# Second-layer output products with the activations as stationary operand and the weights streamed

## The chip, the cores and the metric

The kernel runs on one core of one Trainium2 chip. The metric is the device time of one execution in microseconds, from its first to its last work on the core; the median of three runs is quoted. A program on one core has nothing to exchange with others, so the time is that of the five engines (TensorE, VectorE, ScalarE, GpSimd, SyncE) and their DMA transfers.

## What is computed

A windowed weighted sum over 7 tokens (the "attention"), then two dense layers over 8192 tokens of width 192, each with a hidden width of 2048.

```python
def _moe_ref(x, w_in, w_out):      # first layer
    h = x @ w_in                   # 8192 x 192 @ 192 x 2048
    g = h * np.cos(h)
    return g @ w_out               # 8192 x 2048 @ 2048 x 192

def _moe2_ref(x, w_in, w_out):     # second layer
    h = x @ w_in
    g = np.maximum(0.01 * h, h)
    return g @ w_out

x = attn_out.reshape(8192, 192)
x = _moe_ref(x, w_in1, w_out1)
return _moe2_ref(x, w_in2, w_out2)
```

The weights arrive as 64-bit floats, the activations as 32-bit floats. On the chip every operand of a product is split into a rounded high part and a low remainder ("hi", "lo"), and three products hi x hi, hi x lo, lo x hi are added, so that the sum keeps more bits than one product.

## The kernel before, in words

**Tiling.** The tokens stand in 16 blocks of 512 (four groups of 128, `Q = 4`). The hidden width stands in 16 chunks of 128 (`f`). In both layers activations lie transposed: features on partitions, 512 tokens along the free axis. TensorE is used as two halves of 64 rows (`SIDES`), called side 0 and side 1, each with its own products and weight loads.

**A chunk** (`chunk`, line 819) has 9 *hidden* products (`hidden`, L832: weights loaded, 512 tokens streamed, into one PSUM bank `h`) on the side given by the parity of `f`, then the activation (`acts`), which gives `hi` and `lo` of 128 x 512. In layer 2 that is Prelu in place in the bank (ScalarE, L898), a copy to `hi` (L293, or VectorE) and the difference to `lo` (VectorE, L311); after it the hidden bank is free. In layer 1 the steps are L867, L874, L879, L884 and a difference, most of them on GpSimd.

**Output products** (`project`, L842). A chunk's 128 hidden rows are the contraction; each side takes its 64. Per chunk and side there are five products of 512 columns: the weights `ohi`, `olo` (128 output features) and `or` (the remaining 64, high and low part side by side) are loaded and `hi` or `lo` of 512 tokens streamed. The sums over all 16 chunks stand in two banks per block, `m` and `r`. The result lies transposed, so in layer 2 `take` (line 922) copies the main sum to `om`, adds the halves of the rest to `s` through `sw`, and `back` issues 12 transposes on TensorE (`turn64`, L308) into two banks `po`, which four copies take to `osb`; one store writes the block.

**Order.** `seq` lists all chunks of both layers in pairs; two `streams` alternate at the start. Each side has its list of steps (`lists`): side 0 does the hidden products of pair p and then the output products of pair p - 2, side 1 the output products of pair p - 3 and then the hidden products of pair p. The loop at line 358 puts both lists into one program order, step by step. The two sides must not write one bank at the same time, so where a side turns to a bank that the other side wrote last, at least `APART` steps lie between and a wait (a nop on TensorE, in `piece`) on the end of a product `APART` steps back is put ahead. `Plan` then emits everything engine by engine by due times and costs; the pieces of TensorE's list stay in their order, and every other step goes where its engine is free.

**PSUM.** Eight banks of 128 x 512 float32: hidden banks (`hq`, up to `HELD = 6`), sums (two a block, of two blocks for a while at a change of block) and transposes (`tq`, two). A bank is handed on when its last reader is done.

**Weights** (`weights`, line 689). Four groups of four chunks per layer; each is loaded, taken apart from float64 by ScalarE, VectorE and GpSimd, and split (`ihi`, `ilo`, `ohi`, `olo`, `or`), in the order in which `seq` first needs them.

## Time and profile before

| | |
|---|---|
| median of three runs | 1197.27 us (1196.46 to 1198.04) |
| the profiled execution | 1196.44 us |
| its span, first to last instruction | 1194.6 us |
| TensorE products, busy | 1161.4 us, 97% |
| TensorE weight loads, busy | 1049.5 us, 88% |
| VectorE, ScalarE, GpSimd busy | 75%, 71%, 37% |
| mean granted TensorE clock | 0.988 of full speed |

All numbers but the first row come from one execution under the profiler. Product starts and load times are recorded; a product's end is modelled, and products overlap, so a busy TensorE is judged by the spacing of starts. `PE` is a product, `PEld` a weight load. "x8" behind a row of the timeline means that eight equal instructions were merged into it.

### The profile page before, as it was taken

To read this page: it belongs to the slowest core of one execution; us is meant where nothing else is said; L and a number is where in the kernel's file an instruction comes from. 1 tells how busy PE (TensorE), PEld (TensorE's weight loads), DVE (VectorE), ACT (ScalarE), POOL (GpSimd) and SP (SyncE) were. 2 spreads that over 40 slices of the span, in tenths; PEclk is the share of its full clock that TensorE was granted. 3 is DMA by queue.
4 is the path that set the end of the run, shared out by engine and by line. 5 is a ranking of instruction groups with operands and counts; after the bars stand their busy time and mean duration, and the time that the engine had idled before them with its cause. 6 is when DMAs were issued, how large, how long until landed. Compare 5 with 4: busy or idle time off the path is not lost.

```text
span 1194.6 us, 25907 instructions
## 1 busy us (share of the span) xinstructions
PE 1161.4 (97%) x10364; PEld 1049.5 (88%) x10364; DVE 892.5 (75%) x1356; ACT 852.4 (71%) x1554; POOL 440.3 (37%) x330
## 2 busy tenths in 40 slices
PE   6899799999999999999999999999999999999998
PEld 5677678888888899889998899989999899999997
DVE  7899797888868688786867778787787868746532
ACT  5798657886776767777676766867677676767653
POOL 4685732571432406143250613415052341504200
PEclk8899899999999999999999999999999999999999
DMA  6533420122020121202112120211212012020100
GB/s 180 157 97 89 131 76 15 41 61 54 27 57 18 47 54 63 54 11 62 29 47 55 47 54 2 75 42 48 54 47 54 1 47 54 15 54 15 28 1 27
DMA packets 31334, 62.46 MB, mean 52 GB/s; under 512 B 4276, under 2 KB 22194, under 8 KB 31216
## 3 DMA queue, kind: packets, MB, share of 16 engines
q1 hardware_dynamic: 31216, 60.82, 18.3%
q8 instruction: 82, 1.34, 0.5%
q14 instruction: 36, 0.29, 0.1%
HBM read 30.13 MB, written 6.29 MB: 30 GB/s over the span
## 4 chain that ended last, share of the span: by engine, by line
PE 90%; DVE 3%; DMA 2%; POOL 1%; ACT 1%; issue 1%; SPq 0%; ACTq 0%; DVEq 0%; POOLq 0%
PE ps L842 47%; PE ps L832 41%; PE ps L308 1%; DMA w00out<-in_moe_w_out 1%; DMA w00in<-in_moe_w_in 0%; DVE lo L311 0%; DMA w03in<-in_moe_w_in 0%; POOL ilo L311 0%; DMA x1r<-x1r 0%; ACT hi L293 0%; DVE g L874 0%; ACT g L879 0%; SPq L699 0%; DVE wt00out L754 0%; DVE wt10out L754 0%
## 5 line engine op out<-in xcount | busy, mean ns | idle before, releaser
L311 POOL TENSOR_TENSOR lo<-g,hi 128x512 fp32r<-128x512 f32 x240 | 335.0, 1399 | 517.4 <-ACT hi L293 461.4
L842 PE MATMUL ps<-hi,ohi 64*128 64x512 f32 x1024 | 402.6, 393 | 0.2 <-ACT hi L293 0.2
L842 PE MATMUL ps<-hi,olo 64*128 64x512 f32 x1024 | 398.7, 389 | 3.1 <-POOL olo L311 3.1
L842 PE MATMUL ps<-lo,ohi 64*128 64x512 f32 x1024 | 399.5, 390 | 1.2 <-DVE lo L311 0.6
L842 PE MATMUL ps<-lo,or 64*128 64x512 f32 x1024 | 398.5, 389 | 0.0
L842 PE MATMUL ps<-hi,or 64*128 64x512 f32 x1024 | 397.9, 389 | 0.0
L311 DVE TENSOR_TENSOR lo<-ps,hi 128x512 fp32r<-128x512 f32 x272 | 186.7, 689 | 150.6 <-ACT hi L293 146.1
L898 ACT ACTIVATE ps<-ps 128x512 f32<-128x512 f32 x256 | 148.9, 582 | 143.1 <-PE ps L832 103.0
L884 DVE TENSOR_TENSOR g<-ps,g 128x512 f32<-128x512 f32 x240 | 164.9, 688 | 73.1 <-ACT g L879 68.9
L832 PE MATMUL ps<-x1n,ihi 64*128 64x512 f32 x512 | 199.8, 390 | 2.4 <-DVE x0r L311 2.4
L842 PEld LDWEIGHTS ps<-hi,olo 64*128 64x128 f32 x1024 | 189.3, 185 | 13.8 <-POOL olo L311 3.5
L842 PEld LDWEIGHTS ps<-lo,ohi 64*128 64x128 f32 x1024 | 189.0, 185 | 13.4 <-POOL lo L311 1.7
L832 PE MATMUL ps<-x0n,ihi 64*128 64x512 f32 x512 | 198.9, 394 | 1.3 <-DVE lo L311 1.2
L832 PE MATMUL ps<-x1r,ihi 64*128 64x512 f32 x512 | 199.8, 390 | 0.0
L832 PE MATMUL ps<-x1s,ihi 64*128 64x512 f32 x512 | 198.9, 388 | 0.5 <-DMA x1s<-x1n 0.5
L842 PEld LDWEIGHTS ps<-hi,ohi 64*128 64x128 f32 x1024 | 189.4, 185 | 11.1 <-ACT hi L293 0.5
L832 PE MATMUL ps<-x0r,ihi 64*128 64x512 f32 x512 | 197.3, 389 | 1.8 <-DMA x0r<-x0r 1.8
L842 PEld LDWEIGHTS ps<-hi,or 64*128 64x128 f32 x1024 | 189.4, 185 | 10.8 <-POOL or L311 0.4
L842 PEld LDWEIGHTS ps<-lo,or 64*128 64x128 f32 x1024 | 189.2, 185 | 9.8
L832 PE MATMUL ps<-x0s,ihi 64*128 64x512 f32 x512 | 196.3, 387 | 0.4 <-DMA x0s<-x0n 0.4
L874 DVE SCALAR_TENSOR_TENSOR g<-g,ps 128x512 f32<-128x512 int32 x256 | 174.3, 682 | 26.0 <-ACT g L867 21.3
L879 ACT ACTIVATE g<-g 128x512 f32<-128x512 f32 x256 | 161.4, 632 | 42.8 <-DVE g L874 40.6
(228 smaller groups left out, 2634.9 us busy)
## 6 DMA issues: line engine op xcount, KB each, us to landing
xt<-in_x SPq DMA_DIRECT2D x12, 960.0 KB, 5.1
x1s<-x1n SPq DMA_DIRECT2D x32, 256.0 KB, 3.1
x0s<-x0n SPq DMA_DIRECT2D x30, 256.0 KB, 3.8
out<-osb SPq DMA_DIRECT2D x16, 384.0 KB, 2.7
x0r<-x0r SPq DMA_DIRECT2D x56, 64.0 KB, 3.0
x1r<-x1r SPq DMA_DIRECT2D x56, 64.0 KB, 2.6
smw<-in_weight_gen SPq DMA_DIRECT2D x3, 448.0 KB, 4.1
xt<-in_x SPq DMA_DIRECT2D x3, 384.0 KB, 4.2
```

Of the source, the lines that this page charges most:

```text
L308: nc.tensor.matmul(out, v, ident[r, r.start : r.stop], is_transpose=True, **{"start": True, "stop": True, **flags})
L311: eng[e].tensor_tensor(out=out, in0=a, in1=b.bitcast(F32), op=ALU.subtract)
L832: return nc.tensor.matmul(h(), w[rows, j, d], x()[rows, v], start=i == 0, stop=i == 8)
L842: return nc.tensor.matmul(to(), w[r, f % GF, :], v()[r], start=f == 0 and to_side == 0 and i in (0, 3), stop=f == NF - 1 and to_side == 1 ...
L874: nc.vector.scalar_tensor_tensor(out=g(), in0=g().bitcast(I32), scalar=-2 * math.pi, in1=h(), op0=ALU.mult, op1=ALU.add)
L879: nc.scalar.activation(out=g(), in_=g(), func=AF.Sin, bias=math.pi / 2)
L884: nc.vector.tensor_tensor(out=h() if bank_low else g(), in0=h(), in1=g(), op=ALU.mult)
L898: op(pos + 0.6, {"ACT": 0.58}, lambda e: nc.scalar.activation(out=h(), in_=h(), func=AF.Prelu, alpha=0.01), [kh], [kg], [h])
```

## The change

**Layer 2's output products.** A product now loads 128 tokens' activations (64 hidden rows x 128 columns of `hi` or `lo`) and streams weights. Per chunk, side and group of 128 tokens there are two: `hi` with the high and low weights side by side (384 columns) into columns 0 to 383 of the bank of that token group, and `lo` with the high weights (192 columns) into columns 0 to 191. That is 8 products per chunk and side, 4 of 384 and 4 of 192 columns. Tokens come out on partitions; four banks (one per token group) hold a block's sums. `take_out` copies columns 192 to 383 by ScalarE, adds columns 0 to 191 by VectorE, and stores; `om`, `sw`, `s` and the 12 transposes fall away in layer 2. Layer 1's products and hand-over stay as they are.

**The lists.** Steps now have lengths (512 columns: `MM` = 0.2275, 384: `WIDE`, 192: `NARROW`), each side has a clock, and the step that can start first is put next. `APART` is half a microsecond on these clocks in place of four steps. For a layer-2 pair a side first does the eight `hi` products (token groups 0 to 3 of the first chunk, then of the second), then the eight `lo` products, token group by token group; on side 1 of a block's last pair the second chunk's `hi` come last. **The streams.** The second layer-2 block now follows the first one in the same stream, where they alternated before. **The weights.** Layer 2's output weights of a group are one tile (`ow`) with one copy and one difference in place of two each.

```diff
-    APART = 4
+    APART = 0.5
+    WIDE, NARROW = 0.176, 0.094
...
-    late = [(0, 2), (0, 3)]
+    late = [(1, 1), (0, 2), (0, 3)]
     for b in range(2, NB - 2):
         late += [(1, b), (0, b + 2)]
-    streams = [[(0, 0), (1, 0), *late, (1, NB - 2), (1, NB - 1)], [(0, 1), (1, 1)]]
+    streams = [[(0, 0), (1, 0), *late, (1, NB - 2), (1, NB - 1)], [(0, 1)]]
...
-    OUT = [(j, i) for j in range(2) for i in range(3)] + [(j, i) for j in range(2) for i in (3, 4)]
+    OUT = [
+        [(j, i, "m", j, MM) for j in range(2) for i in range(3)] + [(j, i, "r", 2, MM) for j in range(2) for i in (3, 4)],
+        [(j, ("hi", q), q, j, WIDE) for j in range(2) for q in range(Q)]
+        + [(j, ("lo", q), q, 2, NARROW) for q in range(Q) for j in range(2)],
+    ]
+    OUT.append(OUT[1][:Q] + OUT[1][2 * Q :] + OUT[1][Q : 2 * Q])
+    def outs_of(side, p):
+        _, m, _, f = seq[2 * p]
+        return OUT[2 if m and side and f == NF - 2 else m]
...
+                key = (*seq[2 * p][1:3], out_of(side, step)[2])
+                if side and not i:
+                    if p not in ended:
+                        continue
+                    t = max(t, ended[p] - APART)
+                before = last.get((1 - side, key))
+                if before is not None and before > known:
+                    t = max(t, log[before][0] + APART)
+            if best is None or t < best[0]:
+                best = t, side, step, key
+        t, side, step, key = best
+        kind, p, i = step
+        wait = None
...
+        if key and last.get((1 - side, key), -1) > known:
+            wait = known = max(n for n, x in enumerate(log) if x[0] <= t - APART)
+        clock[side] = t + (out_of(side, step)[4] if key else MM)
...
+        W[m, g] = [wts.tile([P, 2, 3, P], F32R, tag=f"{i}{n}", name=f"{i}{n}") for i in ("ihi", "ilo")]
+        if m:
+            W[m, g] += [wts.tile([P, GF, 2, D], F32R, tag=f"o{n}", name=f"o{n}")]
...
-            acc_of[st] = [bank(f"acc{m}{i}_{b}", None) for i in "mr"]
-        am, ar = acc_of[st]
+            acc_of[st] = [bank(f"acc{m}{i}_{b}", None) for i in (range(Q) if m else "mr")]
...
+            if m:
+                kind, q = i
+                c = slice(q * P, (q + 1) * P)
+                if kind == "hi":
+                    return nc.tensor.matmul(
+                        acc[q]()[:, : 2 * D], ghi()[r, c], ow[0][r, f % GF].rearrange("p a d -> p (a d)"), start=begins, stop=ends)
+                return nc.tensor.matmul(acc[q]()[:, :D], glo()[r, c], ow[0][r, f % GF, 0], start=False, stop=False)
...
+    def take_out(due, b, acc):
+        o = row(f"osb{b}", "osb")
+        k = ("acc", 1, b)
+        for q in range(Q):
+            op(due, {"ACT": 0.34}, lambda e, q=q: copy(e, o()[:, q], acc[q]()[:, D : 2 * D]), [k], [("osb", b, q)], [acc[q], o])
+            op(due + 0.2, {"DVE": 0.37}, lambda e, q=q: nc.vector.tensor_tensor(
+                out=o()[:, q], in0=acc[q]()[:, :D], in1=o()[:, q], op=ALU.add), [k, ("osb", b, q)], [("osb", b, q)], [acc[q], o])
+        op(due + 1, {"SP": 1.35}, lambda e: nc.sync.dma_start(out=of[:, Q * b : Q * b + Q, :], in_=o()),
+           [("osb", b, q) for q in range(Q)], [("out", b)], [o])
...
+        if m:
+            return take_out(due, b, acc)
...
-        o = row(f"osb{b}", "osb")
-        po = [bank(f"po{b}{i}", ("tq", 2)) for i in range(2)]
-        def back(e):
-            for q in range(Q):
-                for i in range(2):
-                    turn64(po[i]()[:, q * R : (q + 1) * R], om()[SIDES[i], q * P : (q + 1) * P], i)
-            for j in range(2):
-                for i in range(2):
-                    turn64(po[i]()[:, HT + j * R : HT + (j + 1) * R], s()[SIDES[i], j * P : (j + 1) * P], i)
-        due += 5
-        op(due, {"PE": 0.66}, back, [("om", m, b), ("s", m, b, 0), ("s", m, b, 1)], [("po", b)], [om, s, *po])
-        for i in range(2):
```

TensorE at the turn from side 0 to side 1 inside a layer-2 block. `hi2` to `lo3` are activations, `ohi`/`olo`/`or` (before) and `o10` (after) layer 2's output weights of group 0, `x1n`, `ihi` the operands of hidden products. In the kernel before:

```order
L842 MATMUL ps2_181<-lo2_616,or10_102 128x512
L832 MATMUL ps7_421<-x1s5_5454,ilo11_104 128x512
L842 MATMUL ps2_181<-hi3_637,or10_102 128x512
L832 MATMUL ps7_421<-x1s5_5454,ihi11_103 128x512
L842 MATMUL ps2_181<-lo3_670,or10_102 128x512
L842 MATMUL ps1_164<-hi2_604,ohi10_100 128x512 [waits PE_49]
L832 MATMUL ps4_380<-x1n5_5426,ihi11_103 128x512 [waits DVE_49]
L842 MATMUL ps1_164<-hi2_604,olo10_101 128x512
```

In the changed kernel:

```order
L875 MATMUL ps4_372<-o10_100,lo4_2123 128x192
L859 MATMUL ps0_123<-x1s6_6997,ihi11_101 128x512
L875 MATMUL ps4_372<-o10_100,lo5_2158 128x192
L875 MATMUL ps5_374<-o10_100,lo4_2123 128x192
L875 MATMUL ps5_374<-o10_100,lo5_2158 128x192
L873 MATMUL ps3_175<-o10_100,hi4_2098 128x384 [waits PE_49]
L859 MATMUL ps2_173<-x1n6_6896,ihi11_101 128x512 [waits DVE_49]
L873 MATMUL ps1_156<-o10_100,hi4_2098 128x384 [waits PE_49]
L859 MATMUL ps2_173<-x1n6_6896,ilo11_102 128x512
L873 MATMUL ps4_372<-o10_100,hi4_2098 128x384 [waits PE_49]
L873 MATMUL ps5_374<-o10_100,hi4_2098 128x384 [waits PE_49]
L859 MATMUL ps2_173<-x1n6_6896,ihi11_101 128x512
```

Where one bank was handed from side to side with one wait on TensorE itself, four are, each with its wait, and narrow products of one side stand in twos and threes between hidden products of the other.

TensorE at a layer-2 block's first output products. In the kernel before (`ps7` is the new sum's bank; the last hidden product on it stands 97 rows earlier):

```order
L842 MATMUL ps4_380<-lo1_532,or03_97 128x512
L842 MATMUL ps7_421<-hi2_604,ohi10_100 128x512 [waits DVE_49]
L832 MATMUL ps0_131<-x1n4_4508,ihi11_103 128x512 [waits DVE_49]
L842 MATMUL ps7_421<-hi2_604,olo10_101 128x512
L832 MATMUL ps0_131<-x1n4_4508,ilo11_104 128x512
L842 MATMUL ps7_421<-lo2_616,ohi10_100 128x512
```

In the changed kernel (`ps3` had its last hidden product 28 rows earlier):

```order
L859 MATMUL ps5_374<-x1n0_3352,ihi11_101 128x512 [waits DVE_49]
L873 MATMUL ps6_411<-o10_100,hi4_2098 128x384 [waits DVE_49]
L873 MATMUL ps0_123<-o10_100,hi4_2098 128x384 [waits DVE_49]
L859 MATMUL ps5_374<-x1n0_3352,ilo11_102 128x512
L873 MATMUL ps7_413<-o10_100,hi4_2098 128x384 [waits DVE_49]
L859 MATMUL ps5_374<-x1n0_3352,ihi11_101 128x512
L873 MATMUL ps3_175<-o10_100,hi4_2098 128x384 [waits DVE_49]
```

Four sums begin within seven rows, each waiting for VectorE to be done with its bank.

GpSimd in the preparation of layer 2's weights (`w12in`: input weights of group 2; L743/L766 clamps, L768/L791 adds, L311/L312 takes a difference). In the kernel before:

```order
L768 TENSOR_TENSOR w12in_1590<-wt12in_1636,w12in_1590 128x768
L768 TENSOR_TENSOR w11out_1409<-wt11out_1573,w11out_1409 128x768
L311 TENSOR_TENSOR ilo12_109<-w12in_1590,ihi12_108 128x768
L311 TENSOR_TENSOR olo11_106<-w11out_1409,ohi11_105 128x512
L311 TENSOR_TENSOR or11_107<-w11out_1409,or11_107 128x4x64
L743 TENSOR_SCALAR wt12out_1734<-wt12out_1734 128x768
```

In the changed kernel:

```order
L791 TENSOR_TENSOR w11out_1325<-wt11out_1561,w11out_1325 128x768
L312 TENSOR_TENSOR o11_103<-w11out_1325,o11_103 128x4x192
L791 TENSOR_TENSOR w12in_1556<-wt12in_1615,w12in_1556 128x768
L312 TENSOR_TENSOR ilo12_105<-w12in_1556,ihi12_104 128x768
L766 TENSOR_SCALAR wt13in_1746<-wt13in_1746 128x768
L766 TENSOR_SCALAR wt12out_1664<-wt12out_1664 128x768
```

Group 3's input weights moved up, ahead of group 2's output weights, and `ilo12` moved behind group 1's output weights.

## Rows read from the trace of the kernel before

**Rows 1.** The page: busy time by engine, and its chain by line.

```profile
PE 1161.4 (97%) x10364; PEld 1049.5 (88%) x10364; DVE 892.5 (75%) x1356; ACT 852.4 (71%) x1554; POOL 440.3 (37%) x330
...
PE ps L842 47%; PE ps L832 41%; PE ps L308 1%; DMA w00out<-in_moe_w_out 1%; DMA w00in<-in_moe_w_in 0%; DVE lo L311 0%; DMA w03in<-in_moe_w_in 0%; POOL ilo L311 0%; DMA x1r<-x1r 0%; ACT hi L293 0%; DVE g L874 0%; ACT g L879 0%; SPq L699 0%; DVE wt00out L754 0%; DVE wt10out L754 0%
```

**Rows 2.** Busy time by stretch: length, engines' busy us, granted clock, DMA share, GB/s.

```profile
165.00:1150.00 985.00, 984.98 (x8844) 901.73 (x8842) 737.72 (x1123) 712.36 (x1304) 333.25 (x240) 1.00 0.15 43
```

**Rows 3.** TensorE's waits from 100 to 165: for whom, total us, times, longest.

```profile
PE ps L832 <- POOL ilo L311: 3.9, 1, 3.9
PE ps L842 <- POOL olo L311: 3.1, 1, 3.1
PE ps L832 <- DVE x0r L311: 2.4, 1, 2.4
```

**Rows 4.** Timeline of TensorE, one half's output products: start, length, engine, line, operation.

```profile
599.63 0.39 PE L842 MATMUL ps<-hi,ohi 64*128 64x512 f32 x1
...
599.86 0.39 PE L842 MATMUL ps<-hi,olo 64*128 64x512 f32 x1
...
601.00 0.39 PE L842 MATMUL ps<-lo,or 64*128 64x512 f32 x1
```

**Rows 5.** Timeline around a block's transposes, one half's hidden products and loads.

```profile
603.75 0.40 PE L832 MATMUL ps<-x0n,ilo 64*128 64x512 f32 x1
...
604.29 0.20 PEld L832 LDWEIGHTS ps<-x0n,ihi 64*128 64x128 f32 x1
...
604.33 0.47 PE L832 MATMUL ps<-x0n,ihi 64*128 64x512 f32 x1
...
604.41 0.19 PEld L832 LDWEIGHTS ps<-x0r,ihi 64*128 64x128 f32 x1
```

**Rows 6.** Timeline near the end, a half that resumes after a pause.

```profile
1185.68 0.18 PEld L842 LDWEIGHTS ps<-hi,ohi 64*128 64x128 f32 x1
1185.68 0.49 PE L842 MATMUL ps<-hi,ohi 64*128 64x512 f32 x1
...
1185.79 0.19 PEld L842 LDWEIGHTS ps<-hi,olo 64*128 64x128 f32 x1
```

**Rows 7.** Timeline of the tail: the last product, eight transposes' loads, the store.

```profile
1187.87 0.39 PE L842 MATMUL ps<-lo,or 64*128 64x512 f32 x1
1188.18 0.33 PEld L308 LDWEIGHTS ps<-ident,om 64*128 64x128 f32 x8 [0.36 <-DVE om L295]
...
1191.28 0.34 SPq L968 DMA_DIRECT2D out<-osb  x1
```

**Rows 8.** Groups by line and shape (count, busy us, mean ns, idle before); last row a wait.

```profile
L293 ACT ACTIVATE hi<-ps 128x512 fp32r<-128x512 f32 x253 | 150.8, 597 | 21.0 <-PE ps L842 7.3 <-DVE ps L884 1.0 <-ACT w13in L762 0.3
L898 ACT ACTIVATE ps<-ps 128x512 f32<-128x512 f32 x256 | 148.9, 582 | 143.1 <-PE ps L832 103.0 <-PE ps L842 36.7
...
L293 ACT ACTIVATE sw<-ps 64x256 f32<-64x256 f32 x60 | 22.7, 379 | 26.4 <-PE ps L842 25.8
...
L293 ACT ACTIVATE osb<-ps 128x128 f32<-128x128 f32 x9 | 2.3, 293 | 0.0
...
L311 DVE TENSOR_TENSOR lo<-ps,hi 128x512 fp32r<-128x512 f32 x272 | 186.7, 689 | 150.6 <-ACT hi L293 146.1 <-PE ps L842 1.5
...
L935 DVE TENSOR_TENSOR s<-ps,sw 64x256 f32<-64x256 f32 x60 | 25.3, 421 | 9.2 <-ACT sw L293 8.2
...
ACT ps L898 <- PE ps L832: 103.0, 133, 1.5
```

**Rows 9.** Timeline of TensorE in the start: products of one half, transposes of the other.

```profile
38.74 0.27 PE L308 MATMUL ps<-ident,pr 64*128 64x64 f32 x1
38.97 0.39 PE L842 MATMUL ps<-hi,olo 64*128 64x512 f32 x1
38.97 0.27 PE L308 MATMUL ps<-ident,pr 64*128 64x64 f32 x1
39.20 0.39 PE L842 MATMUL ps<-lo,ohi 64*128 64x512 f32 x1
```

More of the change, by code (lines that the diff above doesn't have):

```diff
@@ L364, in conv_attention_moe_moe @@
             step = kind, p, i = lists[side][at[side]]
-            if side and kind == "out" and i == 0 and at[0] < len(lists[0]) and lists[0].index(("out", p, 9)) >= at[0]:
-                continue
-            before = last.get((1 - side, bank_of(step))) if kind == "out" else None
-            wait = None
-            if before is not None and before[1] > known:
-                if before[0] > len(steps) - APART:
-                    continue
-                wait = max(n for t, n in log if t <= len(steps) - APART)
-                known = wait
@@ L374, in conv_attention_moe_moe @@
-            log.append((len(steps), len(log)))
-            if kind == "out":
-                last[side, bank_of(step)] = log[-1]
-            now[side] = (step, wait)
-            at[side] += 1
-        steps.append(now)
-    pieces = []
-    for now in steps:
-        key = [x and part(x[0]) for x in now]
-        if not any(key):
-            continue
-        if not pieces or pieces[-1][0] != key:
-            pieces.append((key, []))
-        pieces[-1][1].append(now)
+            t, key = clock[side], None
@@ new lines, in conv_attention_moe_moe @@
+        t, side, step, key = best
[4 more added lines that the diff above has]
+        clock[side] = t + (out_of(side, step)[4] if key else MM)
+        if key:
+            last[side, key] = len(log)
+            if not side and i + 1 == len(outs_of(0, p)):
+                ended[p] = clock[0]
+        log.append((t, side, step, wait))
+        at[side] += 1
@@ L390, in conv_attention_moe_moe @@
+    pieces = []
+    on = [None, None]
+    for x in log:
+        t, side, step, wait = x
+        if on[side] != part(side, step):
+            on[side] = part(side, step)
+            pieces.append([t, []])
+        pieces[-1][1].append(x)
+    ends = [t for t, _ in pieces[1:]] + [max(clock)]
     warm = const.tile([P, 1], F32, name="warm")
@@ L807, in weights @@
                         continue
-                    for j in range(2):
+                    for j in range(2 - m):
                         plan.writers[(n, 2), p, j] = plan.writers[(n, 0), p, j]
@@ L820, in chunk @@
         g4 = f // GF
-        ihi, ilo, ohi, olo, orr = W[m, g4]
+        ihi, ilo, *ow = W[m, g4]
         xn, xs, xr = x_of[m, b]
@@ L972, in conv_attention_moe_moe @@
+        crossed(1, b, due + 1)
+        k = ("s", 1, b, "all")
+        plan.writers[k] = plan.writers["s", m, b, 0] + plan.writers["s", m, b, 1]
+        place(1, b, due + 0.3, k, s)
     op(-90, {"POOL": 1.0}, constants, (), ["ident"])
@@ L991, in conv_attention_moe_moe, with piece @@
     ran = []
-    def piece(key, nows, due):
+    def piece(log, due, cost):
         reads, writes, bufs, then = ["order"], ["order"], [], []
-        for side, at in enumerate(key):
-            if at is None:
-                continue
-            idx = [now[side][0][2] for now in nows]
+        for side, at in {(side, part(side, step)): None for _, side, step, _ in log}:
+            idx = [step[2] for _, s, step, _ in log if s == side and part(s, step) == at]
             if at[0] == "in":
```

126 lines of the change are left out of this document (59 added, 67 removed).

## The prediction

> **What bounds the kernel now.** I read the busy shares first. TensorE is busy for 97% of the span; VectorE and ScalarE follow at 75 and 71% [rows 1]. A share is an average, so the stretches come next: between 165 and 1150 us TensorE is busy for 984.98 of 985.00 us at full clock, and none of its idle time there is listed as a wait [rows 2]. The chain that ended last agrees: 47% of it lies on the line of the output products (L842) and 41% on that of the hidden ones (L832) [rows 1]. So every microsecond put on TensorE's list between 165 and 1184 us, or taken from it, is a microsecond of the span, until another engine's delay reaches TensorE. Before 165 us it does wait, for weights and for one transposed tile [rows 3], and after 1184 us the last block drains.
>
> The array works as two halves of 64 rows, each with its own list of products. One half issues a product of 512 columns every 0.229 us: L842 at 599.63, 599.86, 600.09, ... 601.00 is six steps in 1.37 us [rows 4]. 512 columns at 2.4 GHz are 0.213 us, so 0.016 us is not streaming. For each pair of chunks a half has 9 hidden products and 10 output products, 19 x 0.229 = 4.35 us. Layer 2 has 16 blocks of 8 pairs, 128 pairs.
>
> A product needs its weights in the array, and a load begins when the product before it begins (604.41 in [rows 5], 1185.79 in [rows 6]). A row gives a load 0.18 to 0.20 us, but that is not how long it holds up the next. Look at a half whose weights come late: the load of hi,ohi starts at 1185.68, the next one on that half at 1185.79, while the product reads 0.49 instead of 0.39 us, so it stood about 0.10 us waiting for weights [rows 6]. After the transposes the same pair of loads is 604.29 and 604.41, with the product 0.08 us too long [rows 5]. So loaded weights are ready 0.11 to 0.12 us after the load starts. At 512 columns that is hidden.
>
> **The change part by part.** *Products.* Per pair and half the 10 products of 512 columns become 8 of 384 and 8 of 192; streamed columns fall from 5120 to 4608. No row has either width. The wide one: 160 ns of streaming and the same 16 ns, 0.176 us; it lies between the load's 0.12 and the 0.229 of 512 columns, and is nearest to the latter scaled by its columns (0.172). The narrow one streams 80 ns, less than its load takes. By streaming alone it would be 0.096 us; by the load it is 0.11 to 0.12, at most 0.107 + 0.016 = 0.123. I take 0.115, since [rows 5, 6] show the load itself. Then 9 x 0.229 + 8 x 0.176 + 8 x 0.115 = 4.39 us instead of 4.35, and x 128 = **+4.9 us**; at 0.096 it is -14.6 us, at 0.123 +13.1 us. The saved columns are lost to six more loads per pair and half.
>
> The Trainium skill, page "TensorE: Matmul & The Clock Gate", section "LDWEIGHTS (loading the stationary operand)", gives a load its columns / 1.2 ns, here 107 ns, which speaks against loading activations for 192 columns. Eight loads of the transposes in 0.33 us, four to a half, are some 0.06 us apart [rows 7], so the rule does not hold for these; for the products' loads it does. With 0.107 and no overhead the term would be -3.3 us.
>
> *Transposes back.* Each layer-2 block issued 12 on TensorE. On one half the product before them starts at 603.75, so the next was due at 603.98; it starts at 604.33 and stands 0.08 us for weights, at 604.41 in effect [rows 5]: 0.43 us. 15 blocks have them inside the full stretch: **-6.4 us**. Nothing hid these, since TensorE has no gap there.
>
> *The tail.* Now the last product starts at 1187.87 and the store is issued at 1191.28, 3.4 us later, through sw, s, transposes and copies [rows 7]. After, the four banks' last products start 0.176 us apart. ScalarE copies 192 columns (between 293 ns for 128 and 379 ns for 256 [rows 8], 0.335 us) four times in a row from 0.13 us before the last product starts, and the last VectorE addition (421 ns for 256 columns, so some 0.36 us, and 0.1 us of hand-over) follows: 1.7 us. **-1.7 us**. For the other 15 blocks ScalarE and VectorE lose nine steps (om, two sw, two s, four copies) and get eight of 0.335 and 0.36 us. Both sets lie under TensorE's products, so I cost the difference at nothing; without that cover a block's eight steps would cost the tail's 1.7 us.
>
> *Banks.* There are eight. Layer 2's sums take four instead of two, and its hidden products had up to six. A hidden bank is held from its product (0.39 us) through Prelu, copy and difference (582, 597, 689 ns [rows 8]) with hand-overs, 2.5 us at the least. In the old order the bank that takes a layer-2 block's first output product had its last hidden product 90 or more rows earlier in all but a few blocks; in the new one this is 28 rows in eleven blocks (ps3 before its first 384-column product), and twelve blocks reuse a sum's bank for a hidden product after 28 rows too. 28 rows are about three products and nine more, 2.75 us: 0.25 us to spare. Of its 256 Prelus ScalarE stood idle until the hidden product ended in 133 [rows 8]; in most of the others it was still on something of 0.6 us. What is queued behind the waiting product is all of TensorE, both halves. Some 25 tight places at 0.2 us: **+5 us**; bounds 0 (always just in time) and +14 (40 places, 0.35 us).
>
> *Waits between the halves.* The halves must not write one bank at once, so the list puts a wait on a product's end where the other half was last. Before, that is two waits per half and pair on products 0.9 us older; now four, on products 0.5 us older by the list. The tightest is the fourth wide product, which waits for the first, five rows earlier: started 3 x 0.176 = 0.53 us before; it takes 0.39 - 0.053 = 0.34 us, and a hand-over of 0.06 and a load of 0.115 make 0.51. It fits by 0.02 us. **+2 us**; bounds 0 and 256 x 0.05 = +13 us.
>
> *The start.* The second layer-2 block now follows the first in place of alternating with it, so weight group 3 is due 44 chunks into the list instead of 50, and GpSimd prepares it right after group 2's input weights. TensorE waits there 3.9, 3.1 and 2.4 us now [rows 3]; the last of these, a transposed tile, may vanish, and group 2 may come later. I take 0, bounds -3 and +4.
>
> **Sum.** 4.9 - 6.4 - 1.7 + 5 + 2 + 0 = +3.8 us on the profiled execution's 1196.44 us, so 1200.2 us; the median of the three runs is 0.83 us above that execution, so 1201.0 us. Terms of both signs nearly cancel. Differences below 0.2% (2.4 us) are about what a measurement of this kernel can't tell from no change.
>
> **The rivals.** *Loads hide.* If the narrow products go at 0.096 us because a load can start before its turn, the products give -14.6 us and the sum is -14.6 - 6.4 - 1.7 + 3 (fewer tight waits) = -19.7 us: 1177 to 1178 us. For it: transposes load in half the time [rows 7]. Against it: in [rows 5, 6] the second load of a half starts only when the first one's product does. Chance 0.2.
>
> *Lock-step, the slower side.* While one half runs eight narrow products (0.92 us), the other has three or four hidden products (0.69 us) placed between them. If a product could start only after all that stand ahead of it, the other half would lose time too, and the pair would be two turns of 8 x 0.176 + 8 x 0.115 less one step, 4.54 us: +24.3 us in place of +4.9, 1220 us. It decides from a narrow product of about 0.1 us upwards. Against it: at 38.74 and 38.97 transposes on one half start before the other half's hi,olo (38.97) and lo,ohi (39.20), behind which they stand in the program [rows 9]. So a half can run ahead by a row or two; how far past a wait is open. Chance 0.15.
>
> The Trainium skill, same page, section "Part 3: Packing small matmuls", says that matmuls start and end in program order; that is this rival. Its time by that rule is the 1220 us above; [rows 9] speak against it.
>
> *Banks decide.* If each of the 14 inner blocks loses 1.2 us at its change of banks, +17 instead of +5: 1213 us. Chance 0.12. *Narrow products cost what no row shows*, up to a 512's 0.229 us: 9 x 0.229 + 8 x 0.176 + 8 x 0.229 = 5.30 us a pair, +122 us. Nothing in the rows asks for it: 0.03.
>
> **How the numbers follow.** The forecast, 0.5, spreads over 1193 to 1209 us by itself: a quarter of it lies below 1194.9, somewhat over a quarter within 2.4 us of 1197.3, the rest above. Faster: 0.2 + 0.13 = 0.33. Same: 0.14. Slower: 0.23 + 0.15 + 0.12 + 0.03 = 0.53. For 8 in 10 the range must reach into the first rival and up to the second: 1176 to 1220 us leaves out about half of each and the last one.
>
> **What would show it.** In the changed profile a half's starts of 192-column products stand 0.11 to 0.12 us apart (forecast), 0.09 to 0.10 (loads hide); hidden products beside them keep 0.229 us or stretch to 0.3 and more (lock-step). Idle time of TensorE after 165 us, ended by VectorE, is the banks; ended by TensorE itself, the halves' waits. The transposes of om and s are gone. I am wrong if the pair of layer 2 is under 4.3 us or over 4.5, or if the stretch before 165 us moves by more than 4 us.

## The result and the profile after

The changed kernel takes 1208.81 us (median of 4, 1207.21 to 1210.4) against 1197.65 us for the kernel before on the same chip: ratio 1.0095, 95% interval 1.0077 to 1.0112, so 11.2 us slower. The forecast was 1201.0 us, range 1176 to 1220. Direction and range held; the size was 3.8 us in the sum and 11.2 us on the chip, so something in the sum is too small by some 7 us. The profiled execution of the changed kernel took 1208.15 us, its span is 1206.2 us (before: 1194.6).

The page after, busy time and chain as in [rows 1]:

```profile
PE 1173.0 (97%) x11708; PEld 1120.7 (93%) x11708; DVE 873.4 (72%) x1341; ACT 847.3 (70%) x1549; POOL 428.8 (36%) x326
...
PE ps L859 45%; PE ps L879 21%; PE ps L873 12%; PE ps L875 9%; DMA w00out<-in_moe_w_out 1%; SPq L722 1%; ACT g L918 1%; DVE g L913 1%; PE ps L309 1%; ACT hi L294 0%; DMA w13in<-in_moe_w_in 0%; POOL ilo L312 0%; ACT g L906 0%; DVE lo L312 0%; DMA w03in<-in_moe_w_in 0%
```

L859 are the hidden products, L879 layer 1's output products, L873 the new 384-column ("wide") and L875 the new 192-column ("narrow") ones. TensorE is still the chain, 87% of it on four lines of products. Busy time by stretch (length, busy time and count of PE, PEld, DVE, ACT, POOL; granted clock; DMA share; GB/s), as in [rows 2]:

```profile
0.00:60.00 60.00, 46.78 (x450) 39.48 (x452) 45.36 (x76) 38.54 (x71) 33.55 (x38) 0.80 0.60 156
...
165.00:1150.00 985.00, 984.04 (x9917) 949.61 (x9915) 725.95 (x1119) 702.79 (x1296) 322.65 (x238) 1.00 0.16 43
```

TensorE reads busy for 984.04 of 985 us, 0.94 us less than before. Going by that row, nothing waits. It does: a product's row is 0.25 to 0.39 us long while the next of its half is due after 0.11 to 0.23 us, so a delay of 0.1 or 0.2 us is covered by the row before it and shows only in the starts. I therefore took the starts. The first x1n,ilo product of a layer-2 block, or x0n,ilo of a layer-1 block, dates that block (operation, count, shortest/median/longest ns, first and last start); four blocks of the changed kernel:

```profile
L859 PE MATMUL ps<-x1n,ilo x2: 386/390/394, 107.9 to 109.6; 64*128 64x512 f32 x2
...
L859 PE MATMUL ps<-x1n,ilo x3: 386/388/394, 269.0 to 273.4; 64*128 64x512 f32 x3
...
L859 PE MATMUL ps<-x0n,ilo x3: 383/390/392, 304.7 to 309.1; 64*128 64x512 f32 x3
...
L859 PE MATMUL ps<-x1n,ilo x4: 386/387/392, 1122.0 to 1128.4; 64*128 64x512 f32 x4
```

In this order they are the first layer-2 block, the third, the layer-1 block that follows the third, and the last layer-2 block but one, which the last one follows directly. Read the same way in every kernel (one profiled execution each), they cut the span into five stretches, in us:

| kernel | start to 1st layer-2 block | to the 3rd | one block | steady, 23 blocks | last two blocks and drain | span |
|---|---|---|---|---|---|---|
| before | 105.0 | 160.7 | 35.1 | 808.6 | 85.2 | 1194.6 |
| changed | 107.9 | 161.1 | 35.7 | 817.3 | 84.2 | 1206.2 |
| older | 105.4 | 160.5 | 35.2 | 814.5 | 83.7 | 1199.3 |
| quick0 | 105.3 | 161.2 | 35.7 | 813.5 | 84.3 | 1200.0 |
| quick | 104.8 | 160.0 | 35.2 | 807.5 | 83.7 | 1191.2 |
| b_back2 | 104.4 | 161.9 | 35.1 | 813.0 | 86.0 | 1200.4 |
| b_order | 103.2 | 166.5 | 35.2 | 809.2 | 85.1 | 1199.2 |
| w128 | 104.9 | 162.2 | 35.6 | 817.2 | 83.9 | 1203.8 |
| w256 | 105.9 | 161.4 | 36.3 | 828.2 | 86.1 | 1217.9 |
| n112 | 107.1 | 163.2 | 35.6 | 818.9 | 84.5 | 1209.3 |

Of the 11.6 us between the two spans 8.7 lie in the steady stretch, 2.9 ahead of the first layer-2 block, 1.0 between, and the end gives 1.0 back. The steady stretch has 11 layer-2 blocks and 12 of layer 1; since the outputs of the third layer-2 block lag into it, it has 90 pairs of layer-2 outputs and the hand-overs of 12 layer-2 blocks. The 2.9 us lie where both kernels run layer 1 alone; the granted clock of the first 60 us is 0.80 in this execution of the changed kernel and 0.89 in that of before. The table's other variants of the changed kernel need 104.8 to 107.1 us there, and the one with 107.1 (n112) again has a low clock, 0.86. I don't put these 2.9 us down to the change.

### The profile page after: what moved, and what is told of

It is laid out like the page before. It is cut to its first block, busy times and chain, and to the rows that moved or that the text cites. A ratio compares the mean times of both kernels' runs of the same rounds, so it can differ in the third digit from the quotient of the medians.

```text
span 1206.2 us, 28620 instructions
## 1 busy us (share of the span) xinstructions
PE 1173.0 (97%) x11708; PEld 1120.7 (93%) x11708; DVE 873.4 (72%) x1341; ACT 847.3 (70%) x1549; POOL 428.8 (36%) x326
## 4 chain that ended last, share of the span: by engine, by line
PE 87%; DVE 3%; ACT 3%; issue 2%; DMA 2%; POOL 1%; SPq 1%; DVEq 0%; ACTq 0%; POOLq 0%
PE ps L859 45%; PE ps L879 21%; PE ps L873 12%; PE ps L875 9%; DMA w00out<-in_moe_w_out 1%; SPq L722 1%; ACT g L918 1%; DVE g L913 1%; PE ps L309 1%; ACT hi L294 0%; DMA w13in<-in_moe_w_in 0%; POOL ilo L312 0%; ACT g L906 0%; DVE lo L312 0%; DMA w03in<-in_moe_w_in 0%
## 5 line engine op out<-in xcount | busy, mean ns | idle before, releaser
L312 POOL TENSOR_TENSOR lo<-g,hi 128x512 fp32r<-128x512 f32 x240 | 326.1, 1365 | 531.8 <-ACT hi L294 447.5
L873 PE MATMUL ps<-o,hi 64*128 64x384 f32 x2048 | 421.3, 343 | 7.2 <-DVE lo L312 6.2
L873 PEld LDWEIGHTS ps<-o,hi 64*128 64x128 f32 x2048 | 346.6, 185 | 22.3 <-DVE lo L312 6.9
L312 DVE TENSOR_TENSOR lo<-ps,hi 128x512 fp32r<-128x512 f32 x272 | 187.0, 690 | 166.0 <-ACT hi L294 159.1
L875 PE MATMUL ps<-o,lo 64*128 64x192 f32 x2048 | 264.4, 269 | 0.0
L875 PEld LDWEIGHTS ps<-o,lo 64*128 64x128 f32 x2048 | 264.3, 188 | 0.1
L937 ACT ACTIVATE ps<-ps 128x512 f32<-128x512 f32 x256 | 149.1, 583 | 162.0 <-PE ps L859 103.2
L859 PE MATMUL ps<-x1n,ihi 64*128 64x512 f32 x512 | 205.0, 400 | 1.9 <-DVE lo L312 1.9
L879 PE MATMUL ps<-hi,ohi 64*128 64x512 f32 x512 | 201.9, 394 | 0.2 <-ACT hi L294 0.2
L859 PE MATMUL ps<-x0n,ihi 64*128 64x512 f32 x512 | 200.1, 396 | 1.8 <-DVE lo L312 1.0
L879 PE MATMUL ps<-lo,ohi 64*128 64x512 f32 x512 | 200.3, 391 | 0.7 <-POOL lo L312 0.7
L879 PE MATMUL ps<-hi,or 64*128 64x512 f32 x512 | 200.9, 392 | 0.0
L859 PE MATMUL ps<-x1r,ihi 64*128 64x512 f32 x512 | 200.4, 391 | 0.0
L859 PE MATMUL ps<-x0r,ihi 64*128 64x512 f32 x512 | 199.1, 393 | 1.1 <-DMA x0r<-x0r 1.1
L859 PE MATMUL ps<-x1s,ihi 64*128 64x512 f32 x512 | 200.0, 391 | 0.0
L859 PE MATMUL ps<-x0s,ihi 64*128 64x512 f32 x512 | 198.6, 392 | 1.0 <-DMA x0s<-x0n 1.0
L879 PE MATMUL ps<-hi,olo 64*128 64x512 f32 x512 | 199.2, 389 | 0.0
L879 PE MATMUL ps<-lo,or 64*128 64x512 f32 x512 | 199.2, 389 | 0.0
L918 ACT ACTIVATE g<-g 128x512 f32<-128x512 f32 x256 | 161.1, 631 | 32.1 <-DVE g L913 31.4
L906 ACT ACTIVATE g<-ps 128x512 int32<-128x512 f32 x233 | 138.4, 595 | 52.6 <-PE ps L859 49.5
```

What stands on the lines that cost most here:

```text
L312: eng[e].tensor_tensor(out=out, in0=a, in1=b.bitcast(F32), op=ALU.subtract)
L859: return nc.tensor.matmul(h(), w[rows, j, d], x()[rows, v], start=i == 0, stop=i == 8)
L873: return nc.tensor.matmul(acc[q]()[:, : 2 * D], ghi()[r, c], ow[0][r, f % GF].rearrange("p a d -> p (a d)"), start=begins, stop=ends)
L875: return nc.tensor.matmul(acc[q]()[:, :D], glo()[r, c], ow[0][r, f % GF, 0], start=False, stop=False)
L879: return nc.tensor.matmul(to(), w[r, f % GF, :], v()[r], start=begins and i in (0, 3), stop=ends and i in (2, 4))
L906: nc.scalar.activation(out=k, in_=h(), func=AF.Copy, scale=0.5 / math.pi, bias=0.25)
```

## The experiments

Two suspects stood in the steady stretch: the waits between the halves, and the banks at the turn from one block's sums to the next. A third was the order of the blocks at the start, a fourth the narrow product itself.

**Waits between the halves.** In the changed kernel's list the fourth wide product of a turn waits for the end of the first, five rows earlier. Timeline of TensorE there, products first (start, length, engine, line, operation), then the loads of the wide ones among them:

```profile
655.48 0.34 PE L873 MATMUL ps<-o,hi 64*128 64x384 f32 x1
...
655.66 0.33 PE L873 MATMUL ps<-o,hi 64*128 64x384 f32 x1
...
655.83 0.35 PE L873 MATMUL ps<-o,hi 64*128 64x384 f32 x1
...
656.02 0.39 PE L873 MATMUL ps<-o,hi 64*128 64x384 f32 x1
...
656.25 0.34 PE L873 MATMUL ps<-o,hi 64*128 64x384 f32 x1
```

```profile
655.74 0.18 PEld L873 LDWEIGHTS ps<-o,hi 64*128 64x128 f32 x1
...
655.97 0.18 PEld L873 LDWEIGHTS ps<-o,hi 64*128 64x128 f32 x1
...
656.07 0.19 PEld L873 LDWEIGHTS ps<-o,hi 64*128 64x128 f32 x1
```

The first three start 0.18 us apart. The fourth's load starts only at 655.97, 0.15 us after the first one's row, whose end is modelled, is over (655.48 + 0.34); its product is 0.05 us longer than its like, and the fifth comes 0.23 us after the fourth in place of 0.18. The experiment keeps the order of all products and makes each wait name an older one where an older one will do:

```
-wait = known = max(n for n, x in enumerate(log) if x[0] <= t - APART)
+wait = known = max(last[1 - side, key], *(n for n, x in enumerate(log) if x[0] <= t - OLDER))   # OLDER = 0.75
```

> The changed kernel with the same order of products; only the product that a halves' wait names is an older one (at least 0.75 us before by the list, or the needed one itself), so the fourth 384-column product of a turn waits for the other half's last 192-column product on its bank instead of the first 384-column product five rows ahead. My theory (that wait holds TensorE some 0.05 us, twice in each of 128 pairs): 8 to 13 us faster than the changed kernel's 1208.8, so 1196 to 1201 us, and the fourth wide product starts 0.176 us after the third. Rival (the gap there comes from the loads or from the hidden product that joins, not from the wait): within 1 us of 1208.8, and the gap stays.

It took 1203.25 us, ratio 1.0050 (1.0035 to 1.0065). The gap is gone; the same place in this kernel:

```profile
654.87 0.34 PE L874 MATMUL ps<-o,hi 64*128 64x384 f32 x1
...
655.05 0.33 PE L874 MATMUL ps<-o,hi 64*128 64x384 f32 x1
...
655.22 0.34 PE L874 MATMUL ps<-o,hi 64*128 64x384 f32 x1
...
655.40 0.51 PE L874 MATMUL ps<-o,hi 64*128 64x384 f32 x2
```

A pair with layer-2 outputs fell from 4.43 to 4.37 us (spacing of x1n,ilo, two chunks on), and the time by 5.6 us, less than the 8 to 13 expected: 0.06 us x 128 pairs are 7.7 us, and some of that comes back at the turns (below). The wait was the cause; its size I had put too high this time.

The list's own idea of a narrow product was 0.094 us. Laying it out with the measured one is another way to move the waits:

```
-    WIDE, NARROW = 0.176, 0.094
+    WIDE, NARROW = 0.176, 0.112
```

> The changed kernel with NARROW = 0.112 in place of 0.094, so that the list is laid out with the spacing that the 192-column products show. My theory (only the fourth wide product's wait on one half moves off the first one; the other half's stays): about half of the waits' loss goes, 4 to 6 us faster than 1208.8. Rival (the list being out of step with the chip is itself what costs, since hidden and narrow products then stand in the wrong order): 10 us faster or more.

1210.81 us, ratio 1.0113 (1.0098 to 1.0128): no gain in time, where 4 to 6 or 10 us and more were expected. The steady stretch is 818.9 us. The layer-2 pairs did get shorter, from 4.43 to 4.38 us, so most of the waits' loss there went. But the pairs with layer-1 outputs got longer, from 4.34 to 4.42 us: on either half the second product of a turn, hi,olo, now starts some 0.03 to 0.05 us late, at some 60 turns each. And two turns of blocks stand for 2 us each, for a sum of layer 1 that VectorE reads late. Laying out the list with the measured spacing moved the tight places instead of removing them; why the layer-1 pairs became tight I have not traced.

**The turn of the sums.** The kernel with the older waits has a new, clear place of loss: at eight turns from layer-2 to layer-1 output products (seven by my first count, in the expectation below) TensorE starts nothing for 0.53 us where a product is due after 0.23, always ahead of hi,or. One of them:

```profile
596.46 0.39 PE L860 MATMUL ps<-x0s,ihi 64*128 64x512 f32 x1
596.99 0.50 PE L880 MATMUL ps<-hi,or 64*128 64x512 f32 x1
596.99 0.50 PE L860 MATMUL ps<-x0s,ilo 64*128 64x512 f32 x1
597.33 0.39 PE L880 MATMUL ps<-lo,or 64*128 64x512 f32 x1
```

And what ScalarE, VectorE and GpSimd (POOL) do meanwhile (a row may hold several instructions, x4):

```profile
594.16 1.29 POOL L313 TENSOR_TENSOR lo<-g,hi 128x512 fp32r<-128x512 f32 x1 [0.41 <-ACT hi L295]
...
594.20 1.53 DVE L576 TENSOR_TENSOR xb<-xa,pr 128x256 f32<-128x256 f32 x1
...
594.86 0.97 ACT L295 ACTIVATE osb<-ps 128x192 f32<-128x192 f32 x4
595.66 0.68 DVE L909 TENSOR_SCALAR g<-ps 128x512 int32<-128x512 f32 x1
596.26 0.68 DVE L924 TENSOR_TENSOR g<-ps,g 128x512 f32<-128x512 f32 x1
596.86 0.87 DVE L968 TENSOR_TENSOR osb<-ps,osb 128x192 f32<-128x192 f32 x3
```

hi,or opens layer 1's second sum and needs a bank. In 12 of the 16 blocks, in the changed kernel's program as in this one's, it is the bank of the same block's fourth hidden product. The step that frees it is L924, VectorE's last on that product, and VectorE has a step of the attention (L576, 1.53 us) and one of another product (L909) ahead of it. L924 ends at 596.94 (596.26 + 0.68), hi,or's row begins 0.05 us later, before the first addition of the drain (osb, L968) has ended. The planner takes a hidden product's bank, I think, because the four banks of the sum that has just ended aren't drained: their additions come last. In the changed kernel, same order and same banks, hi,or stands at the same turn from 601.49 to 601.81, 0.3 us where it is some 0.9 us here (due at 596.22, in effect at 597.10): a gain of the older waits is partly handed back.

The difference lies mostly in VectorE's step of the attention. In the changed kernel it is short:

```profile
600.04 0.41 DVE L575 TENSOR_TENSOR xb<-xa,pr 128x256 f32<-128x256 f32 x1
...
600.26 1.34 POOL L312 TENSOR_TENSOR lo<-g,hi 128x512 fp32r<-128x512 f32 x1 [1.89 <-PE ps L859]
```

There GpSimd's difference starts 0.22 us behind VectorE's step; in the kernel with the older waits it starts 0.04 us ahead (594.16), and VectorE's step lasts until 0.28 us after GpSimd's is over. All 14 of these steps take 0.41 or 0.42 us in the changed kernel; with the older waits they take 1.53 us at exactly the eight turns that lose 0.53 us, GpSimd's step being under way each time, and 0.42 us at the other six. No run changes the order of these two steps alone. The experiment makes the drain's eight steps due 8 chunks earlier, on top of the older waits:

```
 def take_out(due, b, acc):
+    due -= 8
```

> The kernel with the older waits, in which the eight steps that drain a layer-2 block's four banks (ScalarE's copies, VectorE's additions) are due 8 chunks earlier, so that VectorE takes them ahead of the attention's and the activations' steps. My theory (at seven turns from layer-2 to layer-1 output products, hi,or waits some 0.6 us for a bank that VectorE's first addition frees behind 1.4 us of other work): the 0.3 us of idle TensorE ahead of hi,or vanish at those turns, 3 to 5 us faster than 1203.25. Rival (the banks are freed by ScalarE's copies or the turn waits for something else, or what VectorE puts off is late next): within 1.5 us of 1203.25.

1195.73 us, ratio 0.9985 (0.9976 to 0.9995): 7.5 us faster than the older waits alone, more than expected, and the only complete kernel here that beats the one before, by 1.3 us. VectorE at the same turn of this kernel, some 3.4 us earlier in the span:

```profile
590.86 1.53 DVE L576 TENSOR_TENSOR xb<-xa,pr 128x256 f32<-128x256 f32 x1
...
592.32 1.14 DVE L969 TENSOR_TENSOR osb<-ps,osb 128x192 f32<-128x192 f32 x4
...
593.38 0.67 DVE L924 TENSOR_TENSOR g<-ps,g 128x512 f32<-128x512 f32 x1
```

My expectation named the wrong releaser (the drain's first addition), and the edit works all the same: the four additions now come ahead of the products' steps, and in eight of the twelve blocks layer 1's second sum takes a drained bank of the sum before, as here: the first addition is over at 592.66, hi,or starts at 592.89, 0.23 us after the product before it. From 165 us to the last product TensorE's starts are never more than 0.27 us apart. The steady stretch is 807.5 us, 1.1 less than before.

The early drain without the older waits:

> The changed kernel with the early drain alone: the eight steps on a layer-2 block's four banks are due 8 chunks earlier, and the halves' waits are as in the change. My theory (the drain's place in the queues and the halves' waits each cost by themselves, some 0.5 us a block and 0.06 us a pair): 6 to 8 us faster than the changed kernel's 1208.8, so 1201 to 1203 us, and the layer-2 pairs keep their 4.43 us. Rival (the drain is late only because the older waits let TensorE reach it sooner): within 2 us of 1208.8.

1202.21 us, ratio 1.0044 (1.0029 to 1.0059), as expected, and the layer-2 pairs stay at 4.43 us. So each costs by itself: the waits, and banks that come free late. By ratios the four kernels stand 11.4 us (changed), 6.0 (older), 5.3 (quick0) and -1.8 us (quick) from the one before: 5.4 us for the waits, 6.1 for the banks (by way of the drain), 13.2 for both.

**The narrow product.** Its starts in the changed kernel, two to a row, with the other half's hidden products (L859) among them:

```profile
655.02 0.39 PE L859 MATMUL ps<-x1s,ilo 64*128 64x512 f32 x1
655.07 0.38 PE L875 MATMUL ps<-o,lo 64*128 64x192 f32 x2
655.25 0.39 PE L859 MATMUL ps<-x1s,ihi 64*128 64x512 f32 x1
655.30 0.38 PE L875 MATMUL ps<-o,lo 64*128 64x192 f32 x2
...
655.52 0.38 PE L875 MATMUL ps<-o,lo 64*128 64x192 f32 x2
```

Four steps in 0.45 us, 0.11 us each, where streaming 192 columns at 2.4 GHz takes 0.08. Two kernels change only what it streams:

```
 return nc.tensor.matmul(acc[q]()[:, :D], glo()[r, c], ow[0][r, f % GF, 0], ...)
w128:   acc[q]()[:, :P],       ow[0][r, f % GF, 0, :P]
w256:   acc[q]()[:, : 2 * P],  ow[0][r, f % GF].rearrange("p a d -> p (a d)")[:, : 2 * P]
```

> The changed kernel whose 192-column products stream only 128 columns; 64 columns of the low products are left out of the sums. My theory (their spacing of 0.1115 us is the load of the next weights, whatever is streamed): within 2 us of the changed kernel's 1208.8, and the spacing stays 0.11 us. Rival (streaming plus a fixed cost sets it): 64 columns less are 0.027 us, x 8 x 128 = 27 us faster, 1182 us.

> The changed kernel whose 192-column products stream 256 columns (64 products of the low parts of activation and weight are added to the sums). My theory (load-bound at 192 columns, and streaming takes over where 256/2.4 = 0.107 us plus 0.008 to 0.016 us exceeds 0.1115): spacing 0.115 to 0.123 us, 4 to 12 us slower than 1208.8. Rival (streaming plus a fixed cost sets it already): 0.027 us more each, 27 us slower, 1236 us.

With 128 columns the spacing is what it was:

```profile
653.01 0.38 PE L875 MATMUL ps<-o,lo 64*128 64x128 f32 x2
653.24 0.38 PE L875 MATMUL ps<-o,lo 64*128 64x128 f32 x2
653.46 0.38 PE L875 MATMUL ps<-o,lo 64*128 64x128 f32 x2
```

and with 256 it is 0.12:

```profile
651.61 0.40 PE L875 MATMUL ps<-o,lo 64*128 64x256 f32 x2
651.85 0.40 PE L875 MATMUL ps<-o,lo 64*128 64x256 f32 x2
652.09 0.39 PE L875 MATMUL ps<-o,lo 64*128 64x256 f32 x2
```

w128 took 1205.09 us (1.0063, 1.0046 to 1.0080). Its steady stretch, 817.2 us, is the changed kernel's to 0.1 us: at 192 columns and fewer the streaming doesn't set the spacing. That the load sets it, and no other fixed part of these products, is argued from the loads' starts in [rows 5, 6]; no run loads fewer columns, and the transposes' loads in [rows 7] follow each other faster. The 3.7 us between the medians, more than the 2 expected, are not there; what the spans differ by lies almost all ahead of the steady stretch, and I leave it open. w256 took 1221.68 us (1.0205, 1.0190 to 1.0221), 12.9 us slower, a little above the 4 to 12 expected; its spacing alone, 0.007 us x 8 x 128, is 7 us. The rest goes by the halves' waits: the fifth wide product of a turn starts 0.50 us after the third (652.58, 653.08) where 0.35 would do and the changed kernel takes 0.42 (655.83, 656.25), and over the steady stretch the wide products are late by some 6 us more on each half than in the changed kernel. Even so it is far from the 27 us of the rival.

**The transposes back.** In the kernel before, each layer-2 block issues its 12 transposes twice:

```
 def back(e):
+    for _ in range(2):
         ... the 12 transposes
```

> The kernel before in which each layer-2 block issues its 12 transposes back twice. My theory (nothing hides them: the prediction's 0.43 us a block is 0.3 us of transposes and some 0.1 us of reloading): 0.3 to 0.43 us more for each of 15 blocks and the tail, 4.5 to 7 us slower than 1197.65. Rival (they fill slots that TensorE has anyway, so that leaving them out gained nothing): within 1 us of 1197.65.

1203.25 us, ratio 1.0047 (1.0030 to 1.0063): 5.6 us by ratio. In the steady stretch it is 4.4 us for the hand-overs of 12 blocks, 0.37 us a block. Nothing hid them.

**The order of the blocks.** The kernel before with the changed order alone:

```
-late = [(0, 2), (0, 3)]
+late = [(1, 1), (0, 2), (0, 3)]
-streams = [[(0, 0), (1, 0), *late, (1, NB - 2), (1, NB - 1)], [(0, 1), (1, 1)]]
+streams = [[(0, 0), (1, 0), *late, (1, NB - 2), (1, NB - 1)], [(0, 1)]]
```

> The kernel before with one part of the change alone: the second layer-2 block follows the first in its stream instead of alternating with it (the three changed numbers in the order of the blocks). My theory (this reordering is what makes the changed kernel's second layer-2 block start 3.3 us later): 3 to 5 us slower than the kernel before's 1197.65, and idle time of TensorE between 100 and 165 us grows by that much. Rival (the loss at the start comes from the new products' four banks and their waits): within 1 us of 1197.65.

1203.05 us, ratio 1.0044 (1.0031 to 1.0058), 5.3 us where 3 to 5 were expected, and the loss sits where expected, between the first and the third layer-2 block: 166.5 instead of 160.7 us. But the changed kernel, with the same order, needs 161.1 us there. So the order costs 5 to 6 us in the old kernel and next to nothing in the new one; what makes up for it there (its layer-2 output weights are split in two pieces a group and not in four) is argued, not shown. Three more kernels, on top of the older waits or of both edits, tried to win time at this place. c4 runs a third layer-1 block ahead of the first layer-2 block (streams [(0, 0), (0, 2), (1, 0), (1, 1), (0, 3), ...] and [(0, 1)]), c2 beside it (streams [(0, 0), (1, 0), (1, 1), (0, 3), ...] and [(0, 1), (0, 2)]), and ahead lets loads and GpSimd's steps start sooner (AHEAD = 24.0 for 16.0):

> The kernel with the older waits, in which layer 1's third block runs ahead of the first layer-2 block, so that layer 2's four groups of weights are due at chunks 48, 52, 56, 60 of the list in place of 32, 36, 40, 44; the order of the rest is kept. My theory (the changed kernel's start is later because layer 2's weights are due before they are split): 3 to 5 us faster than 1203.25, and TensorE's waits for ilo, ihi and lo between 100 and 165 us shrink by that. Rival (the third block's attention and inputs, drawn forward, are late in their turn): no gain, or slower.

> The kernel with the older waits, in which layer 1's third block alternates with the first two layer-2 blocks, so that layer 2's weight groups are due at chunks 36, 40, 44, 50; four banks of layer 2's sums then stand beside two of layer 1's, and two are left for hidden products. My theory of the start (weights due too early) gives 1 to 3 us faster than 1203.25; the rival (banks decide at the start) gives 3 us or more slower, with TensorE waiting for VectorE's lo in that stretch.

> The kernel with older waits and early drain, in which loads and GpSimd's steps may start 24 chunks ahead of their due time in place of 16, so that layer 2's weights can be loaded and split sooner. My theory of the start (GpSimd's steps on the weights come late because they are held back): TensorE's waits for ilo and lo between 100 and 165 us shrink, 2 to 4 us faster than 1195.7. Rival (in the first 165 us the engines that split the weights are taken up by other steps, so a longer lead changes their order and not their end): within 1.5 us of 1195.7, or slower.

c4: 1217.23 us (1.0171, 1.0145 to 1.0196). c2: 1250.3 us (1.0438, 1.0420 to 1.0455). ahead: 1197.82 us (1.0009, 1.0000 to 1.0018), 2 us slower than without it. Weights that are due later are also split later, as the planner works to due times; in c4 TensorE still waits 8.5 us for ilo and 3.3 us for ihi. In c2 it waits for banks (waits from 60 to 200 us: for whom, total, times, longest):

```profile
PE ps L860 <- DVE lo L313: 39.8, 4, 34.2
```

One gap of 34 us. The rows around it:

```profile
153.09 0.59 ACT L938 ACTIVATE ps<-ps 128x512 f32<-128x512 f32 x1
...
177.10 1.07 ACT L295 ACTIVATE hi<-ps 128x512 fp32r<-128x512 f32 x2
...
183.99 1.28 DVE L313 TENSOR_TENSOR lo<-ps,hi 128x512 fp32r<-128x512 f32 x2
...
184.73 0.79 PE L860 MATMUL ps<-x1n,ihi 64*128 64x512 f32 x1 [34.24 <-DVE lo L313]
```

From the Prelu at 153.09 to the copy at 177.10 ScalarE has only steps on layer 2's last two weight groups, and stands up to 7 us at a time for loads and for VectorE; VectorE then has steps of the attention ahead of the difference. So the bank was late because steps on weights and of the attention stood ahead of those that free it; that four banks for the sums would cost this much by themselves is not shown. That my theory of the start named the wrong lever, the due times, is plain from these three.

The rows of the start in the changed kernel point elsewhere:

```profile
122.69 0.90 ACT L763 ACTIVATE wt12in<-w12in 128x768 f32<-128x768 f32 x1 [2.70 <-DMA w12in<-in_moe_w_in]
...
125.52 0.59 ACT L937 ACTIVATE ps<-ps 128x512 f32<-128x512 f32 x1
...
126.63 0.68 DVE L312 TENSOR_TENSOR lo<-ps,hi 128x512 fp32r<-128x512 f32 x1
...
127.37 0.68 PE L873 MATMUL ps<-o,hi 64*128 64x384 f32 x1 [5.20 <-DVE lo L312]
```

ScalarE stands 2.7 us for a load of raw weights, a Prelu is queued behind it (125.52), VectorE's difference behind that (126.63), and TensorE waits 5.2 us for the bank. The load is issued late, since SyncE waits 8.5 us for GpSimd to free one of three raw buffers. The last experiment takes one of GpSimd's steps on each raw tile of layer 2 away:

```
-op(due - 4, {"POOL": 0.17 + 0.44 * w}, clamp, [kt], [kt], [t])
+if m == 0:
+    op(due - 4, {"POOL": 0.17 + 0.44 * w}, clamp, [kt], [kt], [t])
```

> The kernel with older waits and early drain, in which one of GpSimd's three steps on each tile of layer 2's weights is left out: the clamp to the range of exponents (0.83 us on GpSimd for each of eight tiles, with its hand-over between ScalarE and VectorE). My theory of the start (three buffers for raw weights, each freed by GpSimd's last step; the next load lands late, ScalarE stands for it with a Prelu queued behind, and TensorE for the bank): the wait of 5 to 6 us ahead of o,hi at 119 us shrinks, 2 to 5 us faster than 1195.7. Rival (the start is set by the attention's steps or by the halved clock there, not by the weights): within 1.5 us of 1195.7.

1194.08 us, ratio 0.9974 (0.9965 to 0.9984), 1.65 us below quick's median with overlapping intervals. TensorE's two waits ahead of o,hi for a bank fell from 6.8 us in quick to

```profile
PE ps L875 <- DVE lo L313: 2.2, 2, 1.3
```

and the stretch between first and third layer-2 block from 160.0 to 157.4 us. But in the profiled execution the first layer-2 block began 2.8 us later than in quick's (107.6 against 104.8 us, at a clock of 0.86 against 0.91 in the first 60 us), so the third began no earlier (265.0 against 264.8). The chain is supported by the wait and the stretch; by the time, between the 2 to 5 us of the theory and the 1.5 of the rival, it isn't separated from the rival.

## Where the prediction was right, and where not

- **Products, +4.9 us: right.** A narrow product goes at 0.11 us (0.115 taken), a wide one at 0.18 (0.176 taken), and what it streams doesn't set the first (w128). In quick, where both losses are out of the way, the steady stretch is 1.1 us below before; with the 4.4 us of transposes added back that is +3.3 us in 90 pairs, 4.7 in 128.
- **Transposes back, -6.4 us: right.** 0.43 us a block predicted, 0.37 measured for a second set in b_back2, 5.5 us in 15 blocks.
- **The tail, -1.7 us: right.** The last wide product starts at 1201.48 (four in 0.88 us, the last 0.33 long) and the store is issued at 1202.87: 1.4 us in place of 3.4 [rows 7]. ScalarE's copy is 329 ns (0.335 taken), VectorE's addition 345 (0.36 taken):

```profile
1200.93 0.88 PE L873 MATMUL ps<-o,hi 64*128 64x384 f32 x4
1201.32 1.00 ACT L294 ACTIVATE osb<-ps 128x192 f32<-128x192 f32 x4 [7.64 <-PE ps L873]
1201.68 1.15 DVE L967 TENSOR_TENSOR osb<-ps,osb 128x192 f32<-128x192 f32 x4 [7.28 <-ACT osb L294]
1202.87 0.34 SPq L969 DMA_DIRECT2D out<-osb  x1
```

- **Waits between the halves, +2 us: mis-sized; 5.4 by ratio, 7.7 by the pairs.** The place was named to the row (the fourth wide product, the first one's end). The step that failed is "it fits by 0.02 us": it took 0.06 us for the hand-over between the end of one product and the load of the next behind the wait. The rows show 0.15 us to the start of the load alone. With that the wait doesn't fit by 0.07 us, twice a pair; the measured loss is 0.06 us a pair, less than the bound of 13 us; I take it that the other half works on during part of it.
- **Banks, +5 us: right in kind and near in size, 6.1 by ratio; the place was another.** A bank held by a hidden product through its steps on ScalarE and VectorE, reused with no time to spare in a dozen blocks: that is what the runs show. I had put it ahead of a layer-2 block's first wide products. There only two blocks of the steady stretch stand, 1.0 us each, and by the profile for a sum of layer 1 (DVE s) and not for a hidden product. The larger part is at the other turn, ahead of layer 1's hi,or: 0.3 us at each of nine turns. And the lever was one that I had costed at nothing: the drain's eight steps lie under TensorE's products, as the prediction has it, but their place in VectorE's queue decides whether four banks come free before the next sum asks for one.
- **The start, 0: right for the stretch** (161.1 against 160.7 us), but by luck: the order isn't free, alone it costs 5 to 6 us (b_order), and something else in the change makes up for it.
- **Lock-step: no.** Hidden products beside the narrow ones keep their 0.23 us (655.02, 655.25 in the rows above; 598.72, 598.96, 599.19 at an earlier turn). The Trainium skill, page "TensorE: Matmul & The Clock Gate", section "Part 3: Packing small matmuls", has matmuls start and end in program order. The trace doesn't agree for the two halves: the 1220 us of that rule were not reached, and no stretching beside narrow products shows.
- **Loads hide: no.** The narrow products stand 0.11 us apart and not 0.09 to 0.10. The Trainium skill, same page, section "LDWEIGHTS (loading the stationary operand)", would give a load of 128 columns 107 ns. The spacing of 0.11 us agrees with it here.

Put together, products +4.7, transposes -5.5, tail -2.0, waits and banks +13.2 make +10.4 us, of 11.2 measured. The first of these is what quick leaves over, so the sum is no independent check. The forecast of 3.8 us was too small mainly by the waits and banks: 7 us taken, 13.2 measured.

## What to carry to other kernels

When a sum moves into more accumulators, ask who gets their banks next and what stands ahead of the draining steps in their engines' queues; that the drain fits under a busy TensorE doesn't make it free. When a list sets waits by modelled times, let each wait name the oldest product that will do: a tighter one gained nothing here and cost as soon as a hand-over was longer than modelled. And read starts, not busy time: at 984 of 985 us busy this TensorE still lost some 10 us.

## What the chip showed that I had not expected

From the modelled end of a product's row to the load of the product behind a wait on it went 0.15 us (655.82 to 655.97); from the end of VectorE's step to the row of the product that waits for it, 0.05 us (596.94 to 596.99). A narrow product with 128 columns is no faster than one with 192, and one with 256 goes at 0.12 us. A step of VectorE that takes 0.41 us took 1.53 us where a step of GpSimd began 0.04 us ahead of it (594.16, 594.20). Two gains of some 5.4 and 6.1 us gave 13.2 us together in the time, and in the steady stretch of the profiles even 2.8 and 3.8 gave 9.8: with the older waits alone part of the gain went again at the eight turns ahead of hi,or.
